# Low halves of split numbers: a subtraction on GpSimd in place of a product with minus identity in PSUM

## The chip, the core and the metric

The kernel runs on one core of a Trainium2 chip. The metric is device time in microseconds of one execution, the median of several. The core's engines are TensorE (PE, matmuls; PEld is its weight load), VectorE (DVE), ScalarE (ACT), GpSimd (POOL) and SyncE (SP, which only issues DMAs here). Each runs its own instructions in the order in which they are written and waits on semaphores for the others.

## The reference

For 8 batches of 8 heads, 576 rows and head size 64: attention in which each row keeps its 32 largest scores; its output, with the heads side by side, is x (576 x 512 for a batch). Then for each of 4 experts causal attention on projections of x, gated by the two largest of 4 logits.

```python
scores = scale * np.matmul(q, k.transpose(0, 1, 3, 2))
kth = np.partition(scores, -top_k, axis=-1)[..., -top_k:-top_k + 1]
scores = np.where(scores >= kth, scores, -1000000000.0)
attn = softmax(scores)                       # written out in the original
x = heads_side_by_side(np.matmul(attn, v))
...
for e in range(E):
    q, k, v = x @ wq[e], x @ wk[e], x @ wv[e]
    a = softmax(causal(scale * (q @ k.transpose(0, 2, 1))))
    ye = a @ v @ wo[e]
    out += gate[e] * ye                      # the two experts that topk chose
```

All of it is float32. TensorE's fast format here is float32r, a rounded float32; to keep precision the kernel splits a number into a high part (rounded) and a low part (what the rounding left) and adds three products: high by high, low by high, high by low.

## The kernel before

**Stages.** A pair is two heads; there are 32 pairs, four to a batch. For a pair, `prep` loads q and k and splits them; `topk` makes nine score tiles of 128 x 576 in three groups of three and finds each row's 32nd largest score on VectorE (L569 to L608); `stats` makes maxima and sums of the exponentials; `tail` makes transposed scores with the mask added, exponentials, and the attention output (128 x 576, two heads of 64 rows) in the PSUM accumulator. Once per batch `moe` projects the four outputs to v, gate, q and k, and runs the four experts as two pairs of heads (`gp` 0 and 1).

**Where the change sits.** In `tail` the output stands in the accumulator `acc`, of which there is one. ACT copies it into the high part `xb.t[0]` (L809, rounded on writing). Then PE adds the product of minus identity (`negr`) and that high part to the accumulator (L813), so that what is left there is the low part, and ACT copies it into `xb.t[1]` (L815). GpSimd then doubles the last 64 columns of both (L819). In `moe` it is the same for q and k of each `gp`: copy (L983), product with `negr` (L987), copy (L990), with a PSUM tile of the ring `slot` (three tiles). All matmuls go through the helper on L291.

**Buffers.** The v tile of a pair (`vt`, 128 x 640 float32, one tile; its load is on L514) is last used by the output matmuls `av` in `tail`. The output tile of `moe` (`ot`, 128 x 2 x 576 float32, one) is written by L1133 for each `gp` and then split into high (L1140, ACT) and low (L1143, GpSimd). GpSimd also subtracts in `prep` (L471), compares in `topk` (L629) and scales in `moe` (L1093).

**Order.** Nothing is scheduled at run time. Each instruction, or short run of them, is a task with an engine, a cost in ns, dependences and buffers. `Plan.order` simulates the engines, picks at each step the task that can start first, and among those within `SLACK` ns of it the one with the smallest priority: a due time in units of a pair (constants D_...), plus a constant for each kind of task (`BIAS`). Buffers come from rings and are given out in that order. The planner keeps GpSimd's tasks and VectorE's tasks named in `PORT` (instructions with two operands in SBUF) apart in its simulation. On the chip only the `mark` task (L590) holds GpSimd back: it waits for the last two-operand instruction of a group (L586).

Of the kernel before, what the change touches and what calls it, by code (L numbers as in the profile page):

```python
# [101 lines left out]
class Plan:  # L102
# [5 lines left out]
           ("POOL", "SP"): 1400.0, ("DVE", "SP"): 1400.0, ("PE", "SP"): 1400.0}  # L108

    PORT = ("f1", "f3", "f4", "s1", "s7", "ot", "constants", "sub", "low_again")  # L110
    SLACK = 48.1507
    GAP = 160.0


# [115 lines left out]
def act(n, psum=True, ptr=0, accum=0):  # L230
    return 0.833 * max(n, 64) + (51 if psum else 93) + 93 * ptr + 93 * accum
# [6 lines left out]
def pool(n):  # L238
# [2 lines left out]

PEF = 1.0

BIAS = {"<lambda>": 21.16406, "again": 7.086664, "av": 0.291422, "avm": 7.96669, "c1": 6.060996, "c2": -16.917509, "c3":
        -25.219518, "c4": 7.40449, "c5": -35.33028, "cast": 16.673692, "cast_swap": -11.231639, "check1":
        -20.549209, "check2": 47.362819, "check3": -38.010145, "compare": 10.37121, "constants": 3.77208,
        "copy": -5.244973, "count": 19.276636, "diag": 12.150313, "dup": -0.574571, "dup1": -16.263021, "dup2":
# [4 lines left out]
        "load_swap": -1.709559, "loadv": -1.18649, "low_again": -15.590234, "m_stage": -34.500069, "mark":  # L252
        10.382567, "mask": -4.199012, "neg": 9.127403, "neg2": -15.174664, "o_stage": -15.926681, "oh":
        -11.134218, "ol": 20.300811, "ot": -22.486721, "prod": 24.66927, "proj": 0.24706, "rep": -3.538618,
        "s1": -38.259631, "s2": -18.732471, "s3": -11.549524, "s4": -14.828572, "s6": -6.937403, "s7": 7.577078,
        "s8": -2.208531, "s9": -18.824699, "s_stage": 0.053481, "scores": -0.261279, "st": -0.017376, "store":
        -19.029398, "sub": 10.142028, "t_stage": -1.573227, "tails": 9.736612, "vproj": 1.204296, "win":
        18.47031, "xh": 7.127005, "xl": 10.21211}
D_K2 = 29.144853
D_PREP = 2.849825  # L260
D_SC = 0.543928
D_TIE = 11.578646
D_MASK = 1.607309
D_STAT = -3.592427
D_TAIL = 0.282302
D_STEP = 0.102808
D_MOE = 4.208214
D_LAST = 5.999043
D_PEN = 4.17838
D_SPAN = 4.144087  # L270
MP = (14,3)
STO = (0, 1, 5, 2, 6, 3, 7, 8, 4)

# [2 lines left out]
def kernel(ctx, tc, qk, vL, wq, wk, wv, wo, out):  # L276
# [13 lines left out]
    def mm(o, l, r, start=False, stop=False):  # L290
        nc.tensor.matmul(o, l, r, start=start, stop=stop, skip_group_check=True)  # L291
# [143 lines left out]
    def halves(split):  # L435
        return ((0, split), (split, S))
# [307 lines left out]
    def tail(w, shift, xb):  # L744
        acc = Buf(ACC)

        def piece(sl, prt, o0, split, c0, c1, lhsT, r):
            for a, z in ((c0, min(c1, split)), (max(c0, split), c1)):
                if a < z:
                    mm(sl[prt, o0 + a:o0 + z], lhsT, negi[:, r + a - c0:r + z - c0])  # L750

        def st(j, sl):
            split = SPLIT[0] if j < 4 else SPLIT[1]
            o0 = 512 - split
            product(sl.t, o0, split, parts(w, j), (1, 3), (0, 2), False)
            for x, r in parts_of(j):
                if j == 4:
                    prt = slice(64 * x, 64 * x + 64)
                    kc = slice(512, 576) if x == 0 else slice(0, 64)
                else:  # L760
                    prt = al
                    kc = slice(r.start - OFF[x], r.stop - OFF[x])
                c0 = 512 if x == 0 else 0
                piece(sl.t, prt, o0, split, c0, c0 + 64, w.mask[4].t[:, kc], 64 * x)
                for t in range(4):
                    c0 = BASE[x] + t * P
                    piece(sl.t, prt, o0, split, c0, c0 + P, w.mask[t + 5 * x].t[:, kc], 0)

        def av(j, pts):
            v = w.vt.t  # L770
            cs = halves(256)
            if j == 4:
                for c0, c1 in cs:
                    mm(acc.t[:, 256 + c0:256 + c1], v[:, 512:640], pts[0].t[:, c0:c1], stop=True)
            else:
                for x, k in ((0, 0), (1, 0), (1, 1), (0, 1)):
                    c0, c1 = cs[k]
                    mm(acc.t[64 * x:64 * x + 64, 256 + c0:256 + c1], v[:, j * P + x * 64:j * P + x * 64 + 64],
                       pts[x].t[:, c0:c1], start=(j == 0))

        es = {}
        ptb = {}
        w.last_st = []
        for j in STO:
            pl.due = w.p + D_TAIL + D_STEP * len(es)
            sl = Buf(SLOT)
            pt = ptb[j] = Buf(PT)
            x = 0 if j < 4 else 1
            o0 = 512 - (SPLIT[0] if j < 4 else SPLIT[1])
            need = [shift[x], w.k2d[x]] + (w.masked[0:5] if j < 4 else w.masked[4:9])  # L790
            if j == 4:
                need = shift + w.masked + w.k2d
            elif j > 4:
                need.append(shift[0])
            mb = w.mask if j == 4 else (w.mask[0:5] if j < 4 else w.mask[4:9])
            a = add("PE", 767 if j != 4 else 1500, lambda j=j, sl=sl: st(j, sl), need, bufs=[sl, pt] + used(w, j, True) + mb, prio=2, tag="st",
                    kind=MIXED)
            w.last_st.append(a)
            es[j] = add("ACT", act(S), lambda sl=sl, pt=pt, o0=o0: nc.scalar.activation(  # L799
                pt.t, sl.t[:, o0:o0 + S], AF.Exp, scale=0.125), [a], bufs=[sl, pt], prio=1, tag="exp")  # L800
        a = None
        for j in (0, 1, 2, 3, 4):
            jj = [j] if j == 4 else [j, j + 5]
            pts = [ptb[k] for k in jj]
            pl.due = w.p + D_TAIL + D_STEP * (2 * j + 1.5)
            a = add("PE", 1020 if j != 4 else 790, lambda j=j, pts=pts: av(j, pts), [es[k] for k in jj] + [w.v, a],
                    bufs=pts + [acc, w.vt], prio=1, tag="av", kind=SHORT)
        av_ = lambda: acc.t[:, 256:256 + S]
        c = add("ACT", act(S), lambda: nc.scalar.activation(xb.t[0][:, 0:S], av_(), AF.Copy), [a], bufs=[acc, xb], prio=1, tag="xh")  # L809

        def neg():
            for c0, c1 in halves(256):
                mm(acc.t[:, 256 + c0:256 + c1], negr, xb.t[0][:, c0:c1], stop=True)  # L813
        a = add("PE", 250, neg, [c], bufs=[acc, xb], prio=1, kind=LONG)
        d = add("ACT", act(S), lambda: nc.scalar.activation(xb.t[1][:, 0:S], av_(), AF.Copy), [a], bufs=[acc, xb], prio=1, tag="xl")  # L815

        def dup():
            for t in xb.t:
                nc.gpsimd.tensor_copy(t[:, S:640], ft(t[:, 512:S]))  # L819
        return [c, d, add("POOL", 500, dup, [c, d], bufs=[xb], prio=1)]  # L820


    def moe(b, p, xbs, xdone, wd, span, final):
# [41 lines left out]
        for t in range(5):  # L865
# [18 lines left out]
            def ev2(t=t, sl=sl):  # L884
                v.tensor_copy(v2.t[1][:, t], sl.t[:, 256:260])
# [70 lines left out]
        t10 = add("DVE", 100, g10, [t9], bufs=gb, prio=2)  # L956
        gate = add("POOL", 200, g11, [t10], bufs=gb, prio=3)

        done = []
        for gp in range(2):  # L960
            if final and gp:
                clock[0] = fork
# [4 lines left out]
            for name, k in (("q", 0), ("k", 2)):  # L967
# [14 lines left out]
                def ev1(sl=sl, k=k, qk=qk):  # L982
                    nc.scalar.activation(qk.t[k], sl.t[:, o0:o0 + S], AF.Copy)  # L983

                def neg(sl=sl, k=k, qk=qk):
                    for c0, c1 in halves(288):
                        mm(sl.t[:, o0 + c0:o0 + c1], negr, qk.t[k][:, c0:c1], stop=True)  # L987

                def ev2(sl=sl, k=k, qk=qk):
                    nc.scalar.activation(qk.t[k + 1], sl.t[:, o0:o0 + S], AF.Copy)  # L990
                c = add("ACT", act(S), ev1, [a], bufs=[sl, qk], prio=3)
                a = add("PE", 260, neg, [c], bufs=[sl, qk], prio=3, tag="neg2", kind=LONG)
                d = add("ACT", act(S), ev2, [a], bufs=[sl, qk], prio=3)
                ready += [c, d]
                if name == "q":
                    blank_bd = final and gp
# [120 lines left out]
            def av(ts, acc=acc, ptm=ptm, gp=gp):  # L1117
# [13 lines left out]
            when(1900)  # L1131
            a2 = add("PE", 1690, lambda av=av: av((3, 4)), [a1], bufs=[acc, ptm, v2], prio=3, tag="avm", kind=SHORT)
            done.append(add("DVE", dve(S), lambda acc=acc, gp=gp, sm=sm: v.tensor_tensor(  # L1133
                out=ot.t[:, gp], in0=acc.t[:, 0:S], in1=sm.t[2][:, P:P + S], op=OP.mult), [a2, scaled],
                bufs=[acc, ot, sm], prio=2, tag="ot"))
        oo = Buf(QK)
        split = []
        for gp in range(2):
# [3 lines left out]
            def low(gp=gp):  # L1142
                nc.gpsimd.tensor_tensor(out=oo.t[2 + gp], in0=ot.t[:, gp], in1=ft(oo.t[gp]), op=OP.subtract)  # L1143
# [129 lines left out]
```

## Time and profile before

| | |
|---|---|
| median of 3 runs | 1211.62 us (1210.65 to 1213.2) |
| profiled execution | 1211.31 us |
| its span | 1209.5 us |
| mean granted TensorE clock | 0.976 |
| matmuls with minus identity | 64 in `tail`, 60 + 4 in `moe` (the last batch's second half reads another tile) |

The span runs from the first to the last instruction of the program; the rest of the execution lies around it. A busy PE is not PE at its peak, since matmuls overlap in its pipeline and their ends are modelled. Stretches are told in us from the span's start.

### The profile page before, as it was taken

Reading aid. Unit: us, or ns where it says so; the run is one execution under the profiler, and the core shown is the slowest. Engines: PE = TensorE matmul, PEld = TensorE weight load, DVE = VectorE, ACT = ScalarE, POOL = GpSimd, SP = SyncE. Lnnn points to the kernel's source line nnn. Section 1 sums busy time; section 2 is a strip of 40 time slices with the busy share of each in tenths; the row PEclk is TensorE's granted clock in tenths of the full one; section 3 lists DMA queues with packets and bytes.
Section 4 is the critical chain, followed back from the end, with each engine's and each line's share of the span. In section 5 each row is a group of like instructions: output and inputs, shape, how many; then the busy total and the mean of one; then the engine's idle time right before and its main releaser. Section 6 shows DMA issues by size and latency. Waiting matters only on the chain. (4 is left out here: it accounts for less than half of the span.)

```text
span 1209.5 us, 28181 instructions
## 1 busy us (share of the span) xinstructions
PE 1125.3 (93%) x9330; PEld 923.2 (76%) x9330; DVE 1096.4 (91%) x4745; ACT 986.6 (82%) x2050; POOL 378.4 (31%) x803
## 2 busy tenths in 40 slices
PE   3578789999999999999999999999999999999997
PEld 3456668887878778887888878787788878787785
DVE  7999999999999999999999999999999999999121
ACT  5677678899898988979888988989888898888554
POOL 4422222424224332333224232243323333242112
PEclk8688899999999999999999999999999999999999
DMA  7132322224432333333422234323332334220101
GB/s 200 43 90 74 98 74 61 74 72 108 112 86 71 88 90 78 81 91 91 114 81 66 60 98 112 91 66 91 105 76 68 86 99 121 66 71 11 47 5 43
DMA packets 45578, 98.56 MB, mean 81 GB/s; under 512 B 7792, under 2 KB 7792, under 8 KB 45424
## 3 DMA queue, kind: packets, MB, share of 16 engines
q1 hardware_dynamic: 45424, 96.67, 30.0%
q8 instruction: 76, 1.25, 0.4%
q14 instruction: 78, 0.64, 0.2%
HBM read 32.06 MB, written 9.44 MB: 34 GB/s over the span
## 5 line engine op out<-in xcount | busy, mean ns | idle before, releaser
L799 ACT ACTIVATE pt<-slot 128x576 f32<-128x576 f32 x288 | 186.4, 650 | 89.9 <-PE slot L291 88.3
L649 ACT ACTIVATE mask<-s,top 128x576 bf16<-128x576 f32 x288 | 216.4, 772 | 10.6 <-DVE top L603 10.0
L291 PE MATMUL slot<-opa,opa 128*128 128x256 f32 (+3 forms) x984 | 196.1, 326 | 25.1 <-ACT s L558 15.3
L291 PE MATMUL acc<-pt,vt 128*64 128x256 f32 (+3 forms) x1152 | 199.6, 423 | 1.9 <-ACT pt L799 1.9
L291 PEld LDWEIGHTS slot<-opa,opa 128*128 128x128 f32 (+1 forms) x984 | 146.1, 197 | 64.1 <-issue 24.3
L291 PE MATMUL slot<-opb,opb 128*128 128x320 f32 (+1 forms) x960 | 185.7, 314 | 5.9 <-ACT pt L799 2.1
L590 POOL COPY scrap<-cand 128x1 f32<-128x1 f32 x96 | 18.1, 189 | 534.9 <-DVE cand L586 528.3
L558 ACT ACTIVATE s<-slot 128x576 f32<-128x576 f32 x288 | 174.3, 652 | 10.1 <-PE slot L291 9.0
L291 PEld LDWEIGHTS slot<-opb,opb 128*128 128x128 f32 x960 | 141.3, 193 | 22.2 <-issue 11.0
L603 DVE MAX8 top<-cand 128x8 f32<-128x168 f32 x576 | 152.3, 319 | 0.0
L291 PEld LDWEIGHTS acc<-pt,vt 128*64 128x64 f32 (+1 forms) x1152 | 94.5, 143 | 49.8 <-issue 16.3
L577 DVE MAX8 cand<-fb 128x8 f32<-128x288 f32 x288 | 130.4, 453 | 0.0
L291 PE MATMUL slot<-negi,mask 128*128 128x128 bf16 (+3 forms) x1632 | 129.8, 218 | 0.0
L569 DVE TENSOR_TENSOR fa<-s 128x864 f32<-128x864 f32 x96 | 102.7, 1070 | 17.2 <-ACT s L558 16.3
L572 DVE TENSOR_TENSOR fb<-s 128x864 f32<-128x864 f32 x96 | 100.9, 1051 | 0.0
L629 POOL TENSOR_TENSOR ind<-cand,top 128x513 bf16<-128x513 f32 x96 | 100.7, 1049 | 0.1
L291 PEld LDWEIGHTS <-mask 128*128 128x128 bf16 (+1 forms) x1632 | 80.0, 102 | 24.5 <-issue 5.2
L603 DVE MAX8 top<-oct 128x8 f32<-128x72 f32 x576 | 93.6, 216 | 0.0
L608 DVE MATCH_REPLACE8 cand<-top,cand 128x168 f32<-128x168 f32 x288 | 88.6, 317 | 0.0
L637 ACT ACTIVATE ind<-ind,tiny 128x513 bf16<-128x513 bf16 (+1 forms) x96 | 69.7, 726 | 14.3 <-POOL ind L632 7.1
L723 PE MATMUL slot<-identf,stat 128*4 128x128 f32 x288 | 43.1, 278 | 35.6 <-DVE stat L719 28.0
L291 PE MATMUL slot<-opa,k2a 128*128 128x256 f32 (+1 forms) x320 | 70.1, 301 | 1.5 <-ACT opa L727 1.5
(192 smaller groups left out, 2505.9 us busy)
## 6 DMA issues: line engine op xcount, KB each, us to landing
raw<-in_qk_dram SPq DMA_DIRECT2D x31, 576.0 KB, 4.1
opa<-raw SPq DMA_DIRECT2D x93, 144.0 KB, 2.4
opb<-raw SPq DMA_DIRECT2D x93, 144.0 KB, 2.5
vt<-in_vL_dram SPq DMA_DIRECT2D x32, 320.0 KB, 3.1
opa<-opa SPq DMA_DIRECT2D x62, 144.0 KB, 2.4
opb<-opb SPq DMA_DIRECT2D x62, 144.0 KB, 2.9
out_dram<-pr SPq DMA_DIRECT2D x32, 256.0 KB, 2.0
k2a<-opa SPq DMA_DIRECT2D x32, 144.0 KB, 2.3
```

Source lines behind the costliest of these rows:

```text
L291: nc.tensor.matmul(o, l, r, start=start, stop=stop, skip_group_check=True)
L558: nc.scalar.activation(s3.t[:, n], sl.t[:, o0:o0 + S], AF.Copy)
L569: v.tensor_tensor(out=fa.t, in0=s3.t[:, :, 0:288], in1=s3.t[:, :, 288:576], op=OP.max)
L572: v.tensor_tensor(out=fb.t, in0=s3.t[:, :, 0:288], in1=s3.t[:, :, 288:576], op=OP.min)
L577: v.max(out=c.t[:, n, 160:168], in_=fb.t[:, n])
L603: v.max(out=w.top.t[0][:, j, 8 * r:8 * r + 8], in_=oc.t[:, n] if r < 2 else c.t[:, n, 0:168])
L608: v.match_replace(out=c.t[:, n, 0:72] if r == 1 else src, in_values=src, imm_value=LOW, in_to_replace=w.top.t[0][:, j, 8 * r:8 * r + 8])
L629: nc.gpsimd.tensor_tensor(out=ind.t[:, 0:513].rearrange("p (a n) -> p a n", a=3), in0=c.t, in1=m32[:, js[0]:js[0] + 3, 31:32].to_broadcast ...
L637: nc.scalar.activation(ind.t[:, 0:n], ind.t[:, 0:n], AF.Sign, bias=tiny, accum_out=signs[:, 3 * w.p + g:3 * w.p + g + 1])
L649: nc.scalar.activation(w.mask[j].t, s3.t[:, n], AF.Relu, bias=w.top.t[0][:, j, 31:32], scale=-1.0)
L723: nc.tensor.transpose(sl.t[0:4, j * P:(j + 1) * P], ft(parts()[2][:, j]), identf)
L799: es[j] = add("ACT", act(S), lambda sl=sl, pt=pt, o0=o0: nc.scalar.activation(pt.t, sl.t[:, o0:o0 + S], AF.Exp, scale=0.125), [a], bufs=[s ...
```

## The change

The low part is no longer made in PSUM. ACT copies the float32 result out of PSUM a second time, into a float32 scratch, and GpSimd subtracts the high part from the scratch. The scratch is the pair's v tile in `tail` and the output tile in `moe` (`ot[:, 0]` for q of the first half, `ot[:, 1]` for the other three). ACT's second copy depends on the result alone, no longer on the first copy. A copy into `ot` waits for the subtraction that last read the same half (`held`), and the write of `ot` on L1133 waits for both. The last pair's tail and the last batch's q and k keep the product. The planner's constants (`SLACK`, `BIAS`, D_...) all have new values, so the order of all instructions is laid out anew.

```diff
-    SLACK = 48.1507
+    SLACK = 93.2779
...
-        def neg():
-            for c0, c1 in halves(256):
-                mm(acc.t[:, 256 + c0:256 + c1], negr, xb.t[0][:, c0:c1], stop=True)
-        a = add("PE", 250, neg, [c], bufs=[acc, xb], prio=1, kind=LONG)
-        d = add("ACT", act(S), lambda: nc.scalar.activation(xb.t[1][:, 0:S], av_(), AF.Copy), [a], bufs=[acc, xb], prio=1, tag="xl")
+        if w.p == NP - 1 and not w.general:
...
+        else:
+
+            a = add("ACT", act(S), lambda: nc.scalar.activation(w.vt.t[:, 0:S], av_(), AF.Copy), [a],
+                    bufs=[acc, w.vt], prio=1, tag="xl")
+
+            def low():
+                nc.gpsimd.tensor_tensor(out=xb.t[1][:, 0:S], in0=w.vt.t[:, 0:S], in1=ft(xb.t[0][:, 0:S]), op=OP.subtract)
+            d = add("POOL", pool(S), low, [a, c], bufs=[xb, w.vt], prio=1, tag="xs")
...
-        done = []
+        done, held = [], [None, None]
...
+                    z = 1 if k or gp else 0
+
+                    def ev2(sl=sl, z=z):
+                        nc.scalar.activation(ot.t[:, z], sl.t[:, o0:o0 + S], AF.Copy)
+
+                    def low(k=k, qk=qk, z=z):
+                        nc.gpsimd.tensor_tensor(out=qk.t[k + 1], in0=ot.t[:, z], in1=ft(qk.t[k]), op=OP.subtract)
+                    a = add("ACT", act(S), ev2, [a] + held[z:z + 1], bufs=[sl, ot], prio=3)
+                    d = add("POOL", pool(S), low, [a, c], bufs=[qk, ot], prio=3, tag="qs")
+                    held[z] = d
...
-                out=ot.t[:, gp], in0=acc.t[:, 0:S], in1=sm.t[2][:, P:P + S], op=OP.mult), [a2, scaled],
+                out=ot.t[:, gp], in0=acc.t[:, 0:S], in1=sm.t[2][:, P:P + S], op=OP.mult), [a2, scaled] + held,
```

## Rows read from the trace of the kernel before

**Rows 1.** The page's part 1, each engine's busy time, its share of the span and its instructions.

```profile
PE 1125.3 (93%) x9330; PEld 923.2 (76%) x9330; DVE 1096.4 (91%) x4745; ACT 986.6 (82%) x2050; POOL 378.4 (31%) x803
```

**Rows 2.** Busy time of each engine in three stretches; the columns are stretch, its length, then busy us (and instructions) of PE, PEld, DVE, ACT and POOL, the clock granted to PE, the DMA engines' share and GB/s.

```profile
36.00:72.00 36.00, 27.75 (x178) 20.88 (x178) 35.81 (x163) 26.05 (x49) 10.71 (x20) 0.77 0.11 26
...
240.00:1090.00 850.00, 833.07 (x7077) 689.42 (x7076) 827.36 (x3581) 738.46 (x1549) 280.38 (x593) 1.00 0.33 87
...
1110.00:1140.00 30.00, 29.06 (x273) 22.33 (x274) 11.82 (x53) 21.77 (x45) 8.03 (x15) 1.00 0.13 40
```

**Rows 3.** VectorE's groups of instructions from 240 to 1090 us; after the count stand busy us and mean ns, then the idle time before them and what ended it.

```profile
L569 DVE TENSOR_TENSOR fa<-s 128x864 f32<-128x864 f32 x73 | 76.3, 1045 | 11.0 <-ACT s L558 10.1
```

**Rows 4.** Who waited for whom from 240 to 1090 us: total us, times, longest.

```profile
DVE fa L569 <- ACT s L558: 10.1, 6, 1.7
PE slot L723 <- DVE stat L719: 10.0, 13, 0.8
...
DVE v L885 <- ACT v L882: 3.8, 8, 0.6
...
DVE sm L1033 <- PE slot L291: 2.6, 11, 0.3
...
DVE v L885 <- PE slot L291: 1.2, 6, 0.2
```

**Rows 5.** The timeline of PE alone near the end, start us, length us, engine, line, operation, tiles, shape and count (runs of equal instructions are merged).

```profile
1120.22 0.51 PE L291 MATMUL acc<-x,negr 128*128 128x256 f32 x2
1120.67 1.53 PE L291 MATMUL slot<-ptm,v 128*64 128x128 f32 x24
...
1143.56 0.43 PE L291 MATMUL acc<-x,negr 128*128 128x256 f32 x2
1143.82 1.53 PE L291 MATMUL slot<-wo,qk 128*128 128x512 f32 x6
...
1153.48 0.43 PE L291 MATMUL slot<-opa,negr 128*128 128x288 f32 x2
1153.74 1.75 PE L291 MATMUL slot<-x,wk 128*128 128x288 f32 x12
```

**Rows 6.** Groups of the whole span, shapes kept apart: evictions of attention outputs and of q and k, and the subtraction that the output already has.

```profile
L1143 POOL TENSOR_TENSOR qk<-ot,qk 128x576 fp32r<-128x576 f32 x16 | 22.7, 1416 | 10.3 <-ACT qk L1140 10.0
...
L809 ACT ACTIVATE x<-acc 128x576 fp32r<-128x576 f32 x32 | 21.0, 655 | 2.2 <-PE acc L291 2.2
L815 ACT ACTIVATE x<-acc 128x576 fp32r<-128x576 f32 x32 | 20.9, 652 | 0.0
...
L990 ACT ACTIVATE qk<-slot 128x576 fp32r<-128x576 f32 x30 | 19.6, 653 | 2.1 <-PE slot L291 2.1
```

**Rows 7.** The timeline between the load of the v tile for a pair (on the queue of SyncE) and its first use (acc<-pt,vt on PE), with the two copies L809 and L815 of the accumulator, the next group's first instruction on VectorE (L569) and the next mark on GpSimd (L590).

```profile
519.14 0.33 SPq L514 DMA_DIRECT2D vt<-in_vL_dram  x1
...
530.53 0.66 ACT L809 ACTIVATE x<-acc 128x576 fp32r<-128x576 f32 x1
...
533.99 0.65 ACT L815 ACTIVATE x<-acc 128x576 fp32r<-128x576 f32 x1
534.48 1.03 DVE L569 TENSOR_TENSOR fa<-s 128x864 f32<-128x864 f32 x1
...
537.28 1.19 PE L291 MATMUL acc<-pt,vt 128*64 128x256 f32 x8
...
539.25 0.19 POOL L590 COPY scrap<-cand 128x1 f32<-128x1 f32 x1 [7.88 <-DVE cand L586]
```

**Rows 8.** Who waited for whom from 240 to 1090 us, GpSimd's longest.

```profile
POOL scrap L590 <- DVE cand L586: 427.2, 67, 10.1
```

**Rows 9.** Three two-operand instructions of VectorE line by line: count, then ns min/median/max, first and last start.

```profile
L689 DVE TENSOR_TENSOR stat<-top x64: 291/307/782, 34.5 to 1119.4; 128x160 f32<-128x160 f32 x32, 128x128 f32<-128x128 f32 x32
...
L719 DVE TENSOR_TENSOR stat<-stat,stat x64: 154/167/1429, 39.6 to 1122.2; 128x5 fp32r<-128x5 f32 x32, 128x4 fp32r<-128x4 f32 x32
...
L579 DVE TENSOR_TENSOR cand<-fa x96: 591/601/1445, 15.8 to 1109.6; 128x432 f32<-128x432 f32 x96
```

**Rows 10.** The timeline at a place where one of them runs beside an instruction of GpSimd.

```profile
513.26 1.74 POOL L1093 TENSOR_TENSOR sm<-sm,g 128x512 f32<-128x512 f32 x1
514.02 1.45 DVE L579 TENSOR_TENSOR cand<-fa 128x432 f32<-128x432 f32 x1
```

**Rows 11.** Groups of the whole span, shapes kept apart, of VectorE's two-operand instructions and GpSimd's long ones.

```profile
L629 POOL TENSOR_TENSOR ind<-cand,top 128x513 bf16<-128x513 f32 x96 | 100.7, 1049 | 0.1
...
L579 DVE TENSOR_TENSOR cand<-fa 128x432 f32<-128x432 f32 x96 | 63.5, 662 | 0.0
...
L471 POOL TENSOR_TENSOR raw<-raw,opb 128x576 f32<-128x576 f32 x31 | 44.7, 1442 | 69.4 <-ACT opb L462 38.1 <-issue 27.3 <-DVE cand L608 3.3
L471 POOL TENSOR_TENSOR raw<-raw,opa 128x576 f32<-128x576 f32 x31 | 44.1, 1422 | 55.6 <-ACT opa L462 55.6
...
L1093 POOL TENSOR_TENSOR sm<-sm,g 128x512 f32<-128x512 f32 x15 | 20.5, 1366 | 4.3 <-DVE sm L1086 3.7
...
L719 DVE TENSOR_TENSOR stat<-stat,stat 128x4 fp32r<-128x4 f32 x32 | 16.8, 526 | 1.6 <-ACT stat L715 1.5
...
L689 DVE TENSOR_TENSOR stat<-top 128x128 f32<-128x128 f32 x32 | 14.5, 454 | 1.1
```

**Rows 12.** The page's part 6, DMA issues: count, KB each, median us from issue to landing.

```profile
vt<-in_vL_dram SPq DMA_DIRECT2D x32, 320.0 KB, 3.1
```

More of the change, by code (lines that the diff above doesn't have):

```diff
@@ L242 @@
 PEF = 1.0
[L244 to L247, printed above, removed]
[4 rows of a table removed]
[L252 to L270, printed above, removed]
+BIAS = {"<lambda>": 22.930655, "again": 14.257647, "av": 0.260312, "avm": 12.425994, "c1": -1.163119, "c2": -12.784914,
+        "c3": -26.200727, "c4": 7.716813, "c5": -29.926452, "cast": 25.326549, "cast_swap": -9.523144, "check1":
+        -17.854206, "check2": 42.851215, "check3": -37.715299, "compare": 4.048849, "constants": 4.45284,
+        "copy": 1.474971, "count": 26.096157, "diag": 11.460191, "dup": -1.054778, "dup1": -21.499583, "dup2":
[4 rows of a table added]
+        "load_swap": -13.686394, "loadv": 4.267295, "low_again": -15.409371, "m_stage": -39.189602, "mark":
+        0.696374, "mask": -8.126231, "neg": 9.661481, "neg2": -20.777439, "o_stage": -17.455928, "oh":
[3 rows of a table added]
+        -0.252374, "store": -18.372255, "sub": 17.496923, "t_stage": -1.73758, "tails": 8.645462, "vproj":
+        1.106768, "win": 18.936096, "xh": 5.244293, "xl": 13.621857, "xs": -2.513127}
@@ L271 @@
+D_K2 = 31.318306
+D_PREP = 8.874705
+D_SC = -0.206426
+D_TIE = 14.330674
+D_MASK = 8.218923
+D_STAT = -1.065282
+D_TAIL = 0.450827
+D_STEP = 0.092582
+D_MOE = 4.411918
+D_LAST = 7.300807
+D_PEN = 3.622121
+D_SPAN = 3.489439
 MP = (14,3)
@@ L809, in tail, with neg @@
         c = add("ACT", act(S), lambda: nc.scalar.activation(xb.t[0][:, 0:S], av_(), AF.Copy), [a], bufs=[acc, xb], prio=1, tag="xh")
-        def neg():
-            for c0, c1 in halves(256):
-                mm(acc.t[:, 256 + c0:256 + c1], negr, xb.t[0][:, c0:c1], stop=True)
-        a = add("PE", 250, neg, [c], bufs=[acc, xb], prio=1, kind=LONG)
-        d = add("ACT", act(S), lambda: nc.scalar.activation(xb.t[1][:, 0:S], av_(), AF.Copy), [a], bufs=[acc, xb], prio=1, tag="xl")
+        if w.p == NP - 1 and not w.general:
+            def neg():
+                for c0, c1 in halves(256):
+                    mm(acc.t[:, 256 + c0:256 + c1], negr, xb.t[0][:, c0:c1], stop=True)
+            a = add("PE", 250, neg, [c], bufs=[acc, xb], prio=1, kind=LONG)
+            d = add("ACT", act(S), lambda: nc.scalar.activation(xb.t[1][:, 0:S], av_(), AF.Copy), [a], bufs=[acc, xb], prio=1, tag="xl")
+        else:
[4 more added lines that the diff above has]
+            d = add("POOL", pool(S), low, [a, c], bufs=[xb, w.vt], prio=1, tag="xs")
         def dup():
@@ L983, in ev1, with neg, ev2 @@
                     nc.scalar.activation(qk.t[k], sl.t[:, o0:o0 + S], AF.Copy)
[L985 to L990, printed above, removed]
-                c = add("ACT", act(S), ev1, [a], bufs=[sl, qk], prio=3)
-                a = add("PE", 260, neg, [c], bufs=[sl, qk], prio=3, tag="neg2", kind=LONG)
-                d = add("ACT", act(S), ev2, [a], bufs=[sl, qk], prio=3)
+                c = add("ACT", act(S), ev1, [a], bufs=[sl, qk], prio=3)
+                if final:
+                    def neg(sl=sl, k=k, qk=qk):
+                        for c0, c1 in halves(288):
+                            mm(sl.t[:, o0 + c0:o0 + c1], negr, qk.t[k][:, c0:c1], stop=True)
+                    def ev2(sl=sl, k=k, qk=qk):
+                        nc.scalar.activation(qk.t[k + 1], sl.t[:, o0:o0 + S], AF.Copy)
+                    a = add("PE", 260, neg, [c], bufs=[sl, qk], prio=3, tag="neg2", kind=LONG)
+                    d = add("ACT", act(S), ev2, [a], bufs=[sl, qk], prio=3)
+                else:
+                    z = 1 if k or gp else 0
[6 more added lines that the diff above has]
+                    held[z] = d
                 ready += [c, d]
```

11 rows, old and new, of the table BIAS are left out of this document.

## The prediction

> **What bounds the kernel now.** I read the page's engine shares first [rows 1]: TensorE (PE) 93%, VectorE (DVE) 91%, ScalarE (ACT) 82%, GpSimd (POOL) 31%. An average over a start and an end says little, so the table of stretches came next [rows 2]. From 36 to 72 us DVE is busy 35.8 of 36 us and PE only 27.8: the start belongs to DVE. From 240 to 1090 us, six batches, PE is busy 833.1 of 850 us (98.0%) and DVE 827.4 (97.3%): two engines are full at once. After 1110 us DVE is nearly empty and PE is full (29.1 of 30 us from 1110 to 1140): the end belongs to PE.
>
> To get a time for one batch I count the three-tile groups of the search in that window: 73 of them [rows 3], twelve to a batch, so 850 / (73/12) = 139.7 us for a batch. In it DVE works 827.4 / 6.08 = 136.0 us and stands for 3.7; PE works 137.0 and stands for 2.8. The list of waits in the window says what DVE stands for [rows 4]: mostly scores that PE has not yet produced or ACT not yet copied (10.1 us), and the gate's columns of the v projection (3.8 and 1.2) and maxima behind PE (2.6). These four are 17.7 us, 2.9 a batch: DVE waits for the PE side there. PE in turn waits for DVE's statistics (10.0 us). So the question is not whether PE gets lighter, but how much of that becomes DVE's.
>
> **What is removed.** A product with minus identity is two matmuls. The change takes it out of 31 of 32 tails (the last pair keeps it) and of q and k for both head pairs of seven batches of eight, 28: 59 products. In packed stretches the next matmul starts 0.26 us after the product's first one (1143.56 to 1143.82, 1153.48 to 1153.74) [rows 5]; I take this and not the 0.43 us of the row, which includes the last one's run through the pipeline. 59 x 0.26 = 15.3 us of PE; in a steady batch 8 x 0.26 = 2.1 us. Where a narrow product follows, the start moves 0.45 us later (1120.22 to 1120.67), so the upper bound is 3.6 us a batch. No matmul is added.
>
> **What stays equal.** Both ACT evictions remain: the high part as it was, and in place of the low one a float32 copy of the same PSUM tile, into the v tile (tail) or into the output tile (q, k). The old evictions took 655 ns (first) and 652 and 653 (second) [rows 6]; the scratch is float32 where the old target was rounded float32, and I take the same 650 ns, so ACT's time changes by 0 (the unknown part is under the 3 ns by which these groups differ). But the copies no longer wait for PE, so the PSUM slot and the one accumulator come free earlier by about the product and its two hand-overs (in the tail of [rows 7] the first copy ends at 531.19 and the last begins at 533.99). I book no gain of its own for this; it is part of why DVE's waits for scores can shrink.
>
> **What is added.** 59 subtractions of 128x576 on POOL. The kernel has that very instruction for the output's low part: 1416 ns [rows 6]. 59 x 1.42 = 84 us, POOL goes from 378 to 462 us, and 8 x 1.42 = 11.4 us in a batch. POOL has the time: of 850 us it is busy 280 [rows 2] and waits 427 at the mark that holds it back until DVE's two-operand pass over a group is done [rows 8]. The other 143 us, 23.5 a batch, is the room in which 11.4 must go. It fits, at about half.
>
> The price is not POOL's time but DVE's. When a subtraction of POOL runs, a DVE instruction with two SBUF inputs stretches: the 432-wide maximum of L579 takes 0.60 us by its median and 1.45 when POOL's L1093 runs beside it; the subtraction of L689 goes from 0.29 to 0.78 at most, the small one of L719 from 0.15 to 1.43 [rows 9, 10]. The Trainium skill ("SBUF — State Buffer", section on the two separate sides of SBUF) says that the two engines share one pair of ports under an exclusive lock, held for the whole instruction, the loser fully blocked; the trace agrees: that L579 ends 0.47 us after L1093 does, most of its own length, as an instruction that is held and then runs. That rule speaks against the change, and its consequence is the first rival below.
>
> How much of this comes along? Upper bound at today's rate: the groups by form show an excess of (526-160) x 32 + (454-300) x 32 ns on the 4-wide L719 and the 128x128 L689 and (662-601) x 96 on L579 (means of the groups, less lengths between the lines' minimum and median): 11.7 + 4.9 + 5.9 = 22.5 us [rows 9, 11]. It goes with POOL's long two-input instructions, 62 of L471, 16 of L1143, 15 of L1093 and 96 of L629, 88.8 + 22.7 + 20.5 + 100.7 = 232.7 us [rows 6, 11]: 0.097 us of DVE per us of POOL. For 11.4 us that is 1.1 us a batch; lower bound 0, if all lie in the room. The order written for POOL knows DVE's two-operand instructions and puts POOL behind them, and half of the excess is one repeated meeting (L719). I take 0.6.
>
> **The moved waits.** The low part now ends two hops later (copy, then POOL), which delays the duplication of its last columns (L819) and the projections that need all four pairs of a batch; that work is spread over the following four pairs, so nobody stands for it, except in the last batch, where the last pair and q, k keep the product. The v tile is now held until POOL is done, and there is only one; behind it the SP queue has the next pair's v load, 3.1 us to landing [rows 12]. In the stretch shown the load goes out at 519.14, as soon as v's last reader is done, and v is first needed again at 537.28 [rows 7]: 18 us, of which 0.65 x 2 + 1.42 + 3.1 = 5.8 are now needed. Cover is there, if ACT reads the accumulator early; in that tail it reads it only at 530.53. The output tile as a scratch makes k's copy on ACT wait for POOL's subtraction of the q before; the four blocks of k's projection lie between (twelve of their 24 matmuls take 1.75 us in [rows 5]), so 0, and behind it ACT's exponentials would wait if not.
>
> **The sum.** A steady batch: DVE's 2.9 us of waits on the PE side shrink, as PE has 2.1 us less of work; I let half go (1.45), since a PE that is 97% full still delivers late at times, and since the order of all instructions is laid out anew and not only shortened. Contention gives 0.6 back. Net 0.85 a batch. The window holds 6.08 batches and PE is still full at its end; I take 6.4 batches: 5.4 us. At the end, where PE alone sets the time, pair 30's product and what is carried over from the seventh batch go: 1 us. At the start DVE is full and PE is not: 0. That is 1211.3 (the profiled execution; 1209.5 span and 1.8 around it) - 6.4 = 1204.9; the median of 1211.6 is 0.3 above that execution, within the spread of 1210.65 to 1213.2. I say 1205.
>
> Best bound: PE's 2.1 us a batch all become time (PE's wait for DVE does not grow, contention 0): 13.4, with the end and part of the upper price 17: 1194.
>
> **Rivals.** *POOL's lock decides (slower).* Break-even is where collisions eat 1.45 us of DVE a batch; a full one costs 1.43 - 0.15 = 1.28 us [rows 9], so it turns at a little over one of the eight. With two, DVE gets 2.56 us more and 1.45 less: +1.1 x 6.4 = +7, less 1 at the end: 1217. By the rule of the Trainium skill ("SBUF — State Buffer", the two sides of SBUF) this is what each badly placed subtraction does. For it: DVE is 97.3% full, so it has nowhere to put the loss, and the room on POOL is half used up. Against it: L629, the commonest long one, ran 96 times for an excess that is mostly on one small instruction. 15%.
>
> *Nothing comes of it.* DVE's waits for scores stay, because they arise from ACT's order (the releaser is ACT's copy, [rows 4]) and not from PE's load; the lighter PE only stands more. Then 1211, with contention and the end's 1 us cancelling. 17%.
>
> *The v tile (slower).* If ACT still reads the accumulator as late as 530.53, POOL misses the opening that closes at 534.48 (DVE's next group) and subtracts after 539.25 [rows 7], v lands 539.4 + 1.4 + 3.1 = 543.9, 6.6 us after 537.28. With half of that lost once a batch: 3.3 x 6.4 - 6 = +15, 1226. The 11 us by which that read could come earlier speak against it. 6%.
>
> **How the numbers follow.** The forecast, with all its sizes from 1194 to 1209, has 62%. Faster by over 0.2% (about what a measurement can tell from no change) is 0.62, within it 0.17, slower 0.15 + 0.06 = 0.21. The range runs from the best bound, 1194, to the price of two collisions, 1217; beyond lie the v tile and worse collisions on one side and a luckier order on the other.
>
> **What would show it.** Right: PE's busy time falls by about 15 us or more, the groups with minus identity (acc<-x,negr and slot<-qk,negr) shrink by 62 and 56 matmuls, POOL rises by 84 us; in the steady window a group of the search takes less than 139.7 / 12 = 11.64 us and DVE's share rises above 97.3%; DVE's wait for scores (L569) falls under 1.6 us a batch. The lock shows as means of L579, L689 and L719 above those of [rows 11]. Wrong: if DVE's busy time rises by more than 9 us (the first rival), if PE's idle time rises by all that it lost (the second), or if the v load is issued under 4 us ahead of the next use of v (the third).

## The result, and the profile after

The changed kernel takes 1219.01 us (median of 20 runs, 1212.37 to 1226.23) against 1210.66 before (20 runs): a ratio of 1.0063, interval 1.0046 to 1.0080, 0.6% slower where 0.5% faster was forecast. The profiled execution took 1222.68 us, its span 1220.8. The spread is itself a finding: each run comes with the mean clock granted to PE (1 is 2.4 GHz, the upper of its two levels; 0.5 is 1.2 GHz), and the fastest (1212.37 us) had 0.973, the slowest (1226.23) 0.962.

The page after, each engine's busy time and the span in 40 slices (digits are tenths of full clock), answers to [rows 1]:

```profile
PE 1125.7 (92%) x9212; PEld 915.4 (75%) x9212; DVE 1102.4 (90%) x4745; ACT 986.3 (81%) x2050; POOL 467.0 (38%) x862
...
PEclk8788899999999999989999899999999899999999
```

118 matmuls are gone, yet PE is as long busy as before; POOL has 88.6 us more (84 were forecast); DVE has 6.0 us more. The clock line has dips in the middle, where the line of the kernel before has none:

```profile
PEclk8688899999999999999999999999999999999999
```

The table of stretches of the changed kernel, in the columns of [rows 2], shows the same in the middle window and in one piece without a dip and one with; the last two lines are cut at batches (from one batch's first L569 to the next one's): a batch without a dip, and one with.

```profile
240.00:1090.00 850.00, 819.76 (x6846) 669.35 (x6843) 817.91 (x3510) 724.28 (x1523) 342.98 (x623) 0.98 0.32 85
...
360.00:432.00 72.00, 68.04 (x607) 55.78 (x605) 71.28 (x292) 60.47 (x127) 32.87 (x55) 1.00 0.29 76
...
504.00:576.00 72.00, 68.06 (x582) 54.54 (x580) 68.85 (x288) 59.08 (x125) 32.86 (x55) 0.95 0.31 80
...
279.70:420.30 140.60, 135.58 (x1151) 111.23 (x1150) 137.00 (x591) 121.39 (x256) 58.15 (x106) 1.00 0.33 86
563.90:707.10 143.20, 138.24 (x1152) 112.78 (x1151) 137.15 (x590) 121.33 (x256) 58.09 (x106) 0.98 0.32 85
```

The same cut in the kernel before:

```profile
282.50:422.20 139.70, 137.19 (x1169) 113.40 (x1168) 136.15 (x590) 121.62 (x257) 45.69 (x97) 1.00 0.33 88
```

Two things are to be read here. Without a dip, a batch has 1.6 us less of PE (137.19 to 135.58), 0.85 us more of DVE (136.15 to 137.00), and takes 0.9 us longer: it moved with DVE and not with PE (e3 below shows that DVE's time alone does not set it). With a dip it takes another 2.6 us.

What happens at the dip, on the timeline of the changed kernel (GpSimd, then VectorE, then PE; start, length):

```profile
528.19 1.40 POOL L823 TENSOR_TENSOR x<-vt,x 128x576 fp32r<-128x576 f32 x1
529.54 0.41 POOL L828 CAST x<-x 128x64 fp32r<-128x64 f32 x2
...
521.74 2.27 DVE L569 TENSOR_TENSOR fa<-s 128x864 f32<-128x864 f32 x1
...
528.57 1.05 DVE L719 TENSOR_TENSOR stat<-stat,stat 128x4 fp32r<-128x4 f32 x1
...
526.70 1.63 PE L291 MATMUL slot<-opb,opb 128*128 128x256 f32 x8
529.76 0.60 PE L723 MATMUL slot<-identf,stat 128*4 128x128 f32 x4 [1.44 <-DVE stat L719]
...
531.66 0.85 PE L291 MATMUL slot<-opb,opb 128*128 128x320 f32 x2
532.31 0.68 PE L291 MATMUL slot<-opb,k2b 128*128 128x320 f32 x2
...
539.58 0.51 PE L291 MATMUL slot<-opb,opb 128*128 128x320 f32 x2
539.93 0.43 PE L291 MATMUL slot<-opb,k2b 128*128 128x320 f32 x2
```

The tail's new subtraction (L823) runs from 528.19 to 529.59. The subtraction L719, which takes 0.15 us alone, starts at 528.57 and ends at 529.62, when POOL has let go. PE's next instruction is the transposes of those statistics (L723): it stands 1.44 us, where the longest such wait in the window before was 0.8 [rows 4]. Then pairs of matmuls take 0.85 and 0.68 us; the same two forms take 0.51 and 0.43 at 539.6 us. The clock says why (stretches of the same kernel, the granted clock stands behind POOL's column):

```profile
503.80:528.30 24.50, 24.36 (x233) 20.75 (x231) 24.45 (x101) 20.27 (x41) 12.56 (x24) 1.00 0.26 67
528.30:531.60 3.30, 1.86 (x21) 1.41 (x20) 3.30 (x18) 1.41 (x3) 2.75 (x5) 1.00 0.68 164
531.60:538.40 6.80, 6.49 (x35) 4.26 (x31) 5.91 (x25) 4.80 (x16) 1.66 (x3) 0.50 0.33 82
538.40:541.00 2.60, 2.60 (x27) 2.14 (x24) 2.60 (x6) 1.20 (x4) 0.00 (x0) 1.00 0.00 0
```

PE was full and at 2.4 GHz up to 528.3, was busy 1.86 of the next 3.3 us, and then had 1.2 GHz for 6.8 us: 3.4 us of full-speed work lost. It happens at this place in four of the six batches in the window, at a shorter length in a fifth, and by the mean clocks how often it happens differs from run to run. The Trainium skill ("TensorE: Matmul & The Clock Gate", section on HAM oscillation) describes waits between bursts of matmuls behind which the array is throttled again. The trace agrees in kind, not in length: the waits told there are for DMA and of some 3 to 5 us, and here 1.44 us were enough, in five batches of six.

A held L719 is not new, and not enough. In the kernel before, another subtraction of GpSimd (L471) holds it once in every batch, and for longer (GpSimd, VectorE, then PE; the kernel before):

```profile
567.35 1.43 POOL L471 TENSOR_TENSOR raw<-raw,opa 128x576 f32<-128x576 f32 x1
...
567.37 1.43 DVE L719 TENSOR_TENSOR stat<-stat,stat 128x4 fp32r<-128x4 f32 x1
...
567.50 0.69 PE L291 MATMUL slot<-opb,opb 128*128 128x256 f32 x4
568.94 0.60 PE L723 MATMUL slot<-identf,stat 128*4 128x128 f32 x4 [0.75 <-DVE stat L719]
```

There L719 takes 1.43 us, but PE still has matmuls to do up to 568.19, stands only 0.75 us, and its clock stays at 1.00 in the whole window [rows 2]. In the changed kernel PE's last matmul ends at 528.33, 0.24 us before L719 even starts. The difference is what PE has left to do when the hold begins.

The lock's other meetings are in the means, in the columns of [rows 11]:

```profile
L569 DVE TENSOR_TENSOR fa<-s 128x864 f32<-128x864 f32 x96 | 112.9, 1176 | 2.1 <-ACT s L558 2.1
L579 DVE TENSOR_TENSOR cand<-fa 128x432 f32<-128x432 f32 x96 | 58.4, 609 | 0.0
...
L689 DVE TENSOR_TENSOR stat<-top 128x128 f32<-128x128 f32 x32 | 16.4, 513 | 1.1
...
L719 DVE TENSOR_TENSOR stat<-stat,stat 128x4 fp32r<-128x4 f32 x32 | 11.4, 356 | 0.0
```

L569 rises from 1070 ns (the last row below, of the kernel before) to 1176, and the 128x128 L689 from 454 to 513. L579 (662 to 609) and the 4-wide L719 (526 to 356) fall: the new order has also cleared old meetings. In a steady batch four of the eight subtractions meet an instruction of DVE: one of the tails' L719, one L689, and in the second head pair q's L689 and k's L569 (2.27 us above).

```profile
L569 DVE TENSOR_TENSOR fa<-s 128x864 f32<-128x864 f32 x96 | 102.7, 1070 | 17.2 <-ACT s L558 16.3
```

### The profile page after: what moved, and what is told of

The parts are those of the page before. It is cut to its first block, busy times and chain, and to the rows that moved or that the text cites. A ratio compares the mean times of both kernels' runs of the same rounds, so it can differ in the third digit from the quotient of the medians.

```text
span 1220.8 us, 28139 instructions
## 1 busy us (share of the span) xinstructions
PE 1125.7 (92%) x9212; PEld 915.4 (75%) x9212; DVE 1102.4 (90%) x4745; ACT 986.3 (81%) x2050; POOL 467.0 (38%) x862
## 5 line engine op out<-in xcount | busy, mean ns | idle before, releaser
L291 PE MATMUL slot<-opa,opa 128*128 128x256 f32 (+3 forms) x984 | 205.8, 333 | 23.0 <-ACT s L558 12.7
L590 POOL COPY scrap<-cand 128x1 f32<-128x1 f32 x96 | 18.0, 187 | 523.2 <-DVE cand L586 481.4
L291 PE MATMUL acc<-pt,vt 128*64 128x320 f32 (+3 forms) x1152 | 201.5, 425 | 2.0 <-ACT pt L799 1.9
L291 PE MATMUL slot<-opb,opb 128*128 128x320 f32 (+1 forms) x960 | 190.1, 319 | 10.7 <-ACT pt L799 4.4
L569 DVE TENSOR_TENSOR fa<-s 128x864 f32<-128x864 f32 x96 | 112.9, 1176 | 2.1 <-ACT s L558 2.1
L723 PE MATMUL slot<-identf,stat 128*4 128x128 f32 x288 | 44.9, 286 | 36.9 <-DVE stat L719 32.3
L291 PE MATMUL slot<-opb,k2b 128*128 128x320 f32 x320 | 70.7, 303 | 0.2 <-ACT opb L727 0.2
```

Source lines behind the costliest of these rows:

```text
L569: v.tensor_tensor(out=fa.t, in0=s3.t[:, :, 0:288], in1=s3.t[:, :, 288:576], op=OP.max)
L723: nc.tensor.transpose(sl.t[0:4, j * P:(j + 1) * P], ft(parts()[2][:, j]), identf)
```

## The experiments

All ratios are against runs of the kernel before on the same chip. Theory: the tail's subtraction that holds L719 where PE has nothing else to do stops PE, and the clock falls; that is the loss. Rivals: the stretched DVE instructions cost the time themselves; the new constants made a worse order; PE has less work and therefore loses its clock.

| run | us | ratio, interval |
|---|---|---|
| e1_fill | 1212.11 | 1.0009 (0.9998 to 1.0021) |
| e2_late | 1207.25 | 0.9967 (0.9955 to 0.9979) |
| e3_no_sub | 1204.59 | 0.9942 (0.9930 to 0.9955) |
| e4_no_product | 1209.18 | 0.9986 (0.9976 to 0.9996) |
| e5_sub_old_order | 1234.18 | 1.0197 (1.0176 to 1.0218) |
| e6_old_code_new_constants | 1266.22 | 1.0459 (1.0438 to 1.0480) |
| e7_new_code_old_constants | 1257.15 | 1.0396 (1.0368 to 1.0423) |
| e8_no_copy | 1197.61 | 0.9891 (0.9871 to 0.9912) |
| e9_no_tail_sub | 1205.39 | 0.9946 (0.9930 to 0.9962) |
| e10_no_qk_sub | 1219.70 | 1.0067 (1.0041 to 1.0093) |
| e11_hold_statistics | 1212.98 | 1.0012 (1.0002 to 1.0022) |
| e12_late_gp1_product | 1216.25 | 1.0044 (1.0027 to 1.0061) |

**e1: keep PE busy through the wait.** Ten matmuls go ahead of the transposes of L723 in the third pair of each batch (the cut shows the main lines; line numbers are one higher here).

```diff
+        if x == 1 and w.p % 4 == 2:
+            fills.add(t8.n)
...
+        if t.tag == "s8" and t.n in fills:
+            for _ in range(10):
+                mm(acc0[:, 0:256], negr, WT["q"][0][:, 0, 0:256], start=True, stop=True)
         t.fn()
```

> The changed kernel with ten extra matmuls (256 columns each, into columns of the accumulator that nobody reads, about 1.1 us at full clock) issued just ahead of the statistics' transposes of the third pair of each batch, where PE stands 1.44 us waiting for L719. Theory (the wait lets the granted clock fall to 0.5 for 6.8 us, and that is what makes the kernel slower): PE is busy through the wait, the clock stays at 1.00 from 240 to 1090 us, a batch takes 140.5 instead of 143.4 us, the whole 1208 to 1211 us. Rival 1 (the port lock's stretched DVE instructions cost the time themselves, the clock is a side effect): the same as the changed kernel, 1219. Rival 2 (PE is the bound and each matmul counts): 8 x 1.1 us later, 1228.

VectorE and PE at that place, and the middle window:

```profile
526.63 1.07 DVE L720 TENSOR_TENSOR stat<-stat,stat 128x4 fp32r<-128x4 f32 x1
...
526.23 1.30 PE L291 MATMUL acc<-wq,negr 128*128 128x256 f32 x10
527.85 0.60 PE L724 MATMUL slot<-identf,stat 128*4 128x128 f32 x4 [0.32 <-DVE stat L720]
...
240.00:1090.00 850.00, 826.09 (x7033) 679.49 (x7030) 827.66 (x3554) 733.56 (x1541) 350.00 (x636) 1.00 0.32 86
```

PE does useless work for 1.30 us, stands 0.32 us instead of 1.44, and the clock stays at 1.00. 1219.0 becomes 1212.1 (1 us above the expected range) although L719 is held as before (1.07 us) and PE has more to do. The clock alone is worth about 6.9 us; both rivals named there fall.

**e2: take the meeting away.** Only GpSimd's queue changes: in the second pair of each batch (`late` holds these tasks) L823, and what follows from it, goes behind the copy L598.

```diff
+    for t in [x for x in seq if x.n in late]:
+        i = seq.index(t)
+        j = next(k for k in range(i, len(seq)) if seq[k].tag == "tails")
...
+        seq[i:j + 1] = keep + move
```

> The changed kernel, with the tail's subtraction of the second pair of each batch (the one that meets L719) placed behind the copy of the tails (L598) on GpSimd's queue; all else as it was. Theory: L719 runs in 0.16 us instead of 1.05, PE's wait for it falls from 1.44 to under 0.6 us, the clock doesn't fall, 1207 to 1210 us. Rival (less work on PE, not this wait, lets the clock fall): the clock falls as before, 1217 to 1219.

GpSimd, VectorE and PE at the place, the window, and one batch (this kernel's line numbers are one higher at these places):

```profile
528.73 0.20 POOL L599 COPY cand<-cand 128x9 f32<-128x9 f32 x1 [1.37 <-DVE cand L596]
528.89 1.41 POOL L824 TENSOR_TENSOR x<-vt,x 128x576 fp32r<-128x576 f32 x1
...
527.70 0.16 DVE L720 TENSOR_TENSOR stat<-stat,stat 128x4 fp32r<-128x4 f32 x1
...
528.00 0.60 PE L724 MATMUL slot<-identf,stat 128*4 128x128 f32 x4 [0.55 <-DVE stat L720]
...
240.00:1090.00 850.00, 823.31 (x7014) 675.40 (x7011) 826.40 (x3576) 737.03 (x1547) 353.70 (x639) 1.00 0.33 86
...
559.50:699.20 139.70, 135.57 (x1152) 111.18 (x1151) 136.12 (x591) 121.36 (x256) 58.27 (x105) 1.00 0.33 87
```

L719 is back at 0.16 us, PE stands 0.55, the clock holds, and the kernel takes 1207.25 us: 11.8 less than the change as it came and 0.33% less than the kernel before. PE's work is the same as in the changed kernel, so less work on PE is not what lowers the clock. Of the 11.8 us, e1 puts 6.9 down to the clock; the other 4.9 (the wait, the held instruction, what e1's filler itself costs) are not separated. This is the version that beats both.

**e9, e10: one half of the subtractions at a time**, in the changed kernel's order. In e9 ACT's copy of the tail goes into the low half and L823 is not issued; in e10 the same for q and k.

> The changed kernel in its own order without the tails' 31 subtractions (ACT's copy goes straight into the low half, which then holds the whole value); those of q and k stay. Theory (the clock falls only because a tail's subtraction holds L719): no fall of the clock from 240 to 1090 us, 1204 to 1208 us. Rival (all eight subtractions of a batch share the loss): halfway between the changed kernel and the run without any, 1211 to 1213.

> The changed kernel in its own order without the 28 subtractions of q and k (their low half then holds the whole value); the tails' stay. Theory: L719 is still held, PE still stands 1.4 us, the clock still falls in most batches, 1214 to 1219 us; L569 loses its 2.27 us lengths. Rival (the four stretched DVE instructions cost alike): 1211 to 1213.

Their middle windows, e9 first:

```profile
240.00:1090.00 850.00, 823.57 (x7005) 675.29 (x7002) 821.20 (x3585) 737.02 (x1551) 307.50 (x614) 1.00 0.32 86
```

```profile
240.00:1090.00 850.00, 819.67 (x6882) 670.58 (x6881) 809.21 (x3534) 727.83 (x1528) 300.61 (x606) 0.99 0.32 86
```

Without the tails' subtractions 1205.4, without those of q and k 1219.7, no better than with all. The two meetings of q and k (the 2.27 us L569 among them) cost next to nothing: e9, which keeps them, is 0.8 us above e3, and PE's longest wait for the statistics in its middle window is 0.6 us. With e2, it is the meeting with L719 that costs most: 11.8 of the 14.4 us between the changed kernel and e3.

**e3: no subtraction at all, changed order.**

> The changed kernel in its own order, but the 59 subtractions are left out: ACT's second copy goes straight into the low half (which then holds the whole value), GpSimd does nothing. Theory (the lock stretches four DVE instructions of a batch by 0.9 to 1.25 us, one of them stops PE and the clock): DVE's busy time in a batch falls from 137.0 to about 133, no clock falls, a batch takes DVE's time + 3.6 = 136.6 us, the whole about 1187 to 1195. Rival (the new constants made a worse order): 1215 or more.

One batch:

```profile
415.60:555.30 139.70, 135.53 (x1152) 111.19 (x1151) 133.21 (x590) 121.57 (x256) 43.18 (x97) 1.00 0.33 87
```

The clock held in the window and the new order is not a worse one, as the theory said, but its size missed by 10 us: DVE has 3.8 us less in a batch than in the changed kernel's batch without a dip, and the batch is 0.9 us shorter (the next two here, at 140.1, are 0.5 shorter). Relieved of DVE's load it stops there for another reason. So DVE's time is not the bound by itself, and 0.5 to 0.9 us is about all that the lock costs a batch in which the clock does not fall.

**e4: the removal alone, old order.** The products are not issued, nothing else changes.

> The kernel before in its own order, but the 59 products are left out and nothing put in their place (the low half then holds the whole value). Measures what the removal alone is worth. My forecast's step (half of DVE's waits for PE go with PE's work): 1.45 us a batch, about 1200 us. Rival (DVE sets a batch's time, its own busy time + 3.6 us, whatever PE has less): 1208 to 1211. Rival 2 (less work on PE lets the clock fall): over 1214, with granted clock under 1 after 200 us.

```profile
421.90:561.20 139.30, 135.20 (x1151) 111.28 (x1151) 135.96 (x589) 121.35 (x256) 45.66 (x97) 1.00 0.33 86
```

PE has 2.0 us less in a batch, as reckoned, and the batch is 0.4 us shorter (the next one takes 140.3, as before); the whole kernel gains 1.5 us, in the range of the rival and 9 us off the forecast's step. That is what the change had to win in this order.

**e5: the change without its new order.** e4 plus GpSimd's subtraction right behind ACT's copy.

> The kernel before in its own order, the 59 products left out, and in their place GpSimd's subtraction directly behind ACT's second copy (in place in the low half, whose values are then not the low part). The change without its new order. Theory (where a subtraction meets a two-operand instruction of DVE decides): nothing keeps the subtractions out of DVE's way, DVE's busy time rises by 1.1 to 4 us a batch against the run without products, and where the statistics are held the clock may fall: 1211 to 1222 us. Rival (the new order is at fault, not the subtractions): like the run without products, 1209 us.

```profile
429.00:571.60 142.60, 136.79 (x1152) 111.27 (x1152) 139.98 (x589) 121.56 (x256) 59.31 (x105) 1.00 0.32 85
```

25 us more than e4, with the clock at 1.00 in the batch shown: DVE gains 4.0 us a batch, and the batch 3.3. The time is above the expected range, though DVE's gain is that of its upper end. It fits the first rival of the prediction as it was written, through DVE's time; that POOL's own queue, now fuller, has no part in it was not tested.

**e6, e7: constants and code crossed.**

> The code before (products kept) with the changed kernel's constants SLACK, BIAS and D. Theory (the constants as such do no harm; the subtractions do): 1207 to 1213 us, no fall of the clock after 200 us. Rival (the constants make the order worse): 1215 us or more.

> The changed code with the constants before (the two new kinds of task get 0). Theory: subtractions fall where they fall, some on the statistics; 1210 to 1225 us, and the clock falls wherever PE stands over a microsecond for L719. Rival (the new constants are at fault): 1209 us or less.

The theory's numbers miss, by 53 and by 32 us; by its number e6 went to the rival. But the old constants lose as much with the new code as the new ones with the old code, so this is not one set being worse: each serves only the code that it was made for, and an order that does not fit costs 47 to 56 us against the kernel before, more than anything else here. Whether the new order is a good one for the new code is told by e3 and not by these two.

**e8: the second copies left out as well** (the high half is read in place of the low one).

> The kernel before in its own order, the 59 products left out and ACT's 59 second copies too (the high half is read in place of the low one). PE has 2.1 us less a batch, ACT 8 x 0.65 = 5.2 us less. Theory (a batch is set by DVE's time plus what DVE stands for the others): about as without products, 1207 to 1210. Rival (ACT's place in the chain PE - ACT - PE sets the batch): 1.5 us a batch or more, 1198 or less.

```profile
420.60:558.10 137.50, 134.89 (x1152) 111.43 (x1151) 134.65 (x589) 117.68 (x248) 45.68 (x97) 1.00 0.33 88
```

ACT is busy only 118 of 137.5 us, and still 3.7 us less of it takes 1.8 us off a batch, 11.6 off the kernel against e4. The rival's number came out. DVE has 1.3 us less here too (the 4-wide L719 has a mean of 298 ns against 521 in e4), so ACT's place in the chain is likely, not proved.

**e11: hold the statistics in the kernel before**, by one more subtraction on GpSimd.

> The kernel before, products kept, with one more subtraction on GpSimd (128 x 576, into a tile that nobody reads) in the third pair of each batch, started by the same logarithm that releases L719. Theory (a held L719 stops PE for over a microsecond and the granted clock falls to 0.5, with PE's work unchanged): L719 takes 1.3 us there, PE stands 1.5 us or more, the clock falls after 200 us in most batches; 8 x (1.2 + up to 3.4) = 10 to 37 us more than before. Rival (the clock falls in the changed kernel because PE has less work): no fall, at most 8 x 1.2 = 10 us more.

Inconclusive. The subtraction had four casts ahead of it on GpSimd's queue and came late:

```profile
528.71 1.06 POOL L1010 CAST bd<-qk 64x64 fp32r<-64x64 f32 x4
529.92 1.15 POOL L718 TENSOR_TENSOR hold<-hold,stat 128x576 bf16<-128x576 bf16 x1
```

PE's longest wait for the statistics in the middle window stayed at 0.8 us, so the theory was not put to the test here. The kernel before, with its L719 held 1.43 us and no fall of the clock, already says that the hold alone is not enough; a wait of 1.44 us with the products kept stands in no run.

**e12: e2 with the product back for q and k of the second head pair.**

> The run with the late tail subtraction (1207.25 us), and the q and k of the second head pair get the product with minus identity back (they are the two whose subtractions meet L689 and L569). DVE has about 2.2 us a batch less, PE 0.5 more. If DVE's time sets the batch: 1207 - 7 x 1.7 = 1195. If the order of PE and ACT sets it at 139.7 us, as in the run without subtractions (1204.6): 1205 to 1208.

```profile
560.70:702.70 142.00, 137.65 (x1156) 112.19 (x1155) 134.58 (x591) 121.47 (x256) 55.96 (x104) 1.00 0.33 86
```

Neither: 1216.25. DVE has 1.5 us less than in e2 and the batch is 2.3 us longer (139.7 there), with the clock at 1.00. PE has 2.1 us more, where 0.5 were expected. DVE now stands for ACT instead: 23.9 us in the middle window for the exponentials of L701, against 2.9 in e2. A likely reason is that the product stands between ACT's two copies again, in an order that leaves it no room; no run isolates it. That DVE's time sets the batch is refuted for this order a second time.

## Why the prediction was wrong

**The step that failed** is the price of the lock in "What is added": "The price is not POOL's time but DVE's." The prediction had the wait of PE for L719 in [rows 4] (10.0 us) and the lengths of L719 in [rows 9] (0.15 to 1.43 us), and put "PE's wait for DVE does not grow" among the conditions of its best bound; yet it priced a held L719 at 1.28 us of DVE. Its price is what PE does behind it: it stands 1.44 us and then, mostly, runs at half clock for 6.8. e2 takes this one meeting away and wins 11.8 us; e1 leaves the meeting and fills the wait, and wins 6.9. The granted clock was in [rows 2], at 1.00, and was given no price. The rest of the sum had the right sign: the new order without subtractions (e3) is 6.1 us faster than the kernel before, the other meetings take back 2.7 (e2 less e3), and the 3.4 us left are e2's gain, where 6.4 were forecast; the one meeting turned that into 8.4 us lost. The prediction also took L719's excess in the kernel before for one repeated meeting; there are two in a batch (0.6 and 1.43 us), and PE stands 0.75 us at the longer.

**The gain was mis-sized.** 0.26 us for a product was right (PE has 2.0 us less a batch in e4, against 2.1), but "I let half go (1.45)" was not: the batch became 0.4 us shorter at most, the kernel 1.5 us. Waits between PE, ACT and DVE in a fixed order did not shrink with PE's work. For the removal alone the sum had 1.45 x 6.4 and 1 at the end, 10.3 us; it was 1.5 in the old order (e4) and 6.1 in the new one (e3). "Nothing comes of it" (17%) would have been the result for the old order with the subtractions free.

**The contention was about right as a sum** (DVE +0.85 us a batch against 0.6, between the bounds 0 and 1.1), though as a balance: four meetings of about 1 us each came, and old ones went.

**The first rival** (15%) had the right cause, the lock, and the wrong path: it counted meetings of any kind against DVE's 1.45 us. By e9 and e10 it depends on which instruction is met. That its 1217 lies near 1219 is luck; e5 is closer to the case as written.

**The rest.** ACT's copies cost the same (657 and 649 ns for the new ones). POOL had room for the work. No wait of PE for the v tile's load stands in the changed kernel's list, though the third rival's sign came once, near the end (the load issued at 1101.35, v used at 1104.86). Of the other signs, "DVE's busy time rises by more than 9 us" did not come (6.0), so it would not have told; PE's busy time "falls by about 15 us" did not either, because half clock lengthened what was left (in e2 it falls by 11.5, to 1113.8). One sign of being right came and told nothing: DVE's wait for scores went from 10.1 us in the window to none, but all its waits together from 20.0 to 30.7, now mostly behind ACT's copies of v (L894, 12.2) and a step of POOL on the sums (L1108, 9.9).

**Open:** what holds a batch at about 140 us when DVE and PE are both relieved (e3). e8 and e12 point to the alternation of ACT and PE; no run isolates it. Open too is why the same wait lowers the clock in one batch and not in another.

## What to carry to other kernels

When work goes to GpSimd, list the VectorE instructions with two SBUF inputs that it can meet, and for each one who waits for it: a 0.15 us subtraction that gates TensorE is dearer to hold than a 1 us one that nobody stands for, and it is dear where TensorE has no other matmuls queued (held 1.43 us and harmless before, held 1.05 us and costly after). Price a new TensorE wait twice, for its length and for the clock that may fall behind it. And between two engines that are 97 and 98% full in a fixed order, taking 2 us from one of them is not 2 us, nor half of it, until a run with only that removal says so.

## What the runs showed that I had not expected

The same 1.44 us wait lowered the clock in some batches and not in others (the one at 387.4 us left it at 1.00), and so a fixed program ran from 1212.4 to 1226.2 us; the kernel before, without the wait, spread over 7 us, and the six of e2 over 2 (1206.03 to 1207.99). In e4 PE stood up to 1.1 us at a time for the same statistics, and the middle window had the clock at 1.00. And useless matmuls, 80 of them in the whole kernel, made it 6.9 us faster.
